# Linear attention with two MLP layers on one core: a new order of the opening and of the first block, k scaled by GpSimd, three gate buffers

## The chip, the core and the metric

The kernel runs on one core of a Trainium2 chip. A core has TensorE (matmuls, here PE; its weight loads are PEld), VectorE (DVE), ScalarE (ACT), GpSimd (POOL) and SyncE (SP, which here only issues DMAs). The metric is the device time of one execution in microseconds (us); smaller is better.

## The reference

Eight heads of a linear attention with a decaying state over 768 positions and four batches, then two MLPs on the 3072 tokens of 384 features, with 2048 hidden units each:

```python
for t in range(S):
    state = alpha[:, :, t, :, None] * state + np.einsum('bhd,bhe->bhde', k[:, :, t], v[:, :, t])
    y[:, :, t] = np.einsum('bhd,bhde->bhe', q[:, :, t], state)
# x = y as (tokens, heads * head_dim)
h = x @ w_in;  g = h * (1.0 / (1.0 + np.exp(-1.702 * h)));  x = g @ w_out
h = x @ w_in2; g = h - np.tanh(h);                          out = g @ w_out2
```

## The kernel before

**Attention.** It works in 24 chunks of 128 positions (4 batches of 6), g = 0 to 23. For a chunk VectorE makes two running products of alpha (`a_scan`, lines 258 and 261) and multiplies k by the one (line 265) and q by the other (line 266), in `a_scale`. TensorE makes the scores in two parts (`s_mm`, line 294, banks 5, 6, 3 and 4); ScalarE copies them out (line 306, and the turned k at line 303) and GpSimd masks them (line 308); then TensorE makes the outputs (`a_out`, lines 356 and 349) and the step of the state (`a_delta`, line 370), which VectorE adds (`a_state`). ScalarE copies the outputs (`a_evac`, line 414), DMAs take them to memory and back in the MLP's layout (`a_back`, line 429), and ScalarE and VectorE split them into a high and a low part (`x_hi`, line 436, and `x_lo`, line 440). A guard (`a_guard`, line 270) squares the running products on ScalarE. Chunks 2 and 3 of the opening go round the memory: placing matrices, copied by GpSimd out of the identity (`a_picks`, line 396), lay them by TensorE (`a_lay`, line 400).

**MLPs.** 3072 tokens are six blocks of 512 for each layer; a block is 16 steps, one for each 128 hidden units. A step is nine matmuls `gemm1` (line 453; high x high, high x low, low x high of three pieces of 128 features), an activation on ScalarE into a gate buffer (`gf`, in layer 1 line 467), its split into `ghi` (line 470) and `glo`, and, three steps later, nine matmuls `gemm2` (line 460). Steps are s = 0 to 191. In the first block the low part is made by ScalarE's negated copy (line 472) and a DMA that GpSimd issues and that adds the gate buffer to it (line 473); later VectorE makes it (line 475). Step s uses gate buffer s mod 2.

**Weights.** 64-bit weights of a step come by DMA (`given`, line 162). VectorE makes a 32-bit number of them (`w_bits`, lines 172 and 173, and `w_join`, line 185); ScalarE rounds it to the high part (`w_hi`, line 204) and VectorE subtracts for the low part (`w_lo`, line 208).

**The order.** Every engine works its instructions in the order in which the program writes them (`in_order` pins this for layer 1's first blocks). The opening computes chunks 0 to 3 and the weights of steps 0 and 1, with `idle` matmuls as fill (line 613). The first block then carries chunks 4 to 7 with it: one of three parts of a chunk (scores, scores, outputs) in each step from step 2, a weight in each step (`conv`: the low part of one weight, then the join of the next, then the bits of the one after), and the chunk's guard.

## Time and profile before

| | us |
|---|---|
| median of 3 runs | 932.02 (929.82 to 932.99) |
| the profiled execution | 934.48, its span 932.80 |
| TensorE busy | 912.6 (98%) |
| VectorE busy | 661.1 (71%) |
| ScalarE busy | 454.6 (49%) |
| GpSimd busy | 107.5 (12%) |

The profile is of one execution. Its page has busy times, the span in 40 slices of 23.3 us, and the granted clock of TensorE in tenths; beside it the trace answers with timelines (an x16 behind a row says how many instructions of one kind are merged in it; the first number is the start of the first, the second the busy time of all), waits, and a table by stretches of time. A busy TensorE is not one at its peak: matmuls are pipelined, and at half the granted clock the same matmul lasts longer.

### The profile page before, as it was taken

To read this page: it belongs to the slowest core of one execution; us is meant where nothing else is said; L and a number is where in the kernel's file an instruction comes from. 1 tells how busy PE (TensorE), PEld (TensorE's weight loads), DVE (VectorE), ACT (ScalarE), POOL (GpSimd) and SP (SyncE) were. 2 spreads that over 40 slices of the span, in tenths; PEclk is the share of its full clock that TensorE was granted. 3 is DMA by queue.
4 is the path that set the end of the run, shared out by engine and by line. 5 is a ranking of instruction groups with operands and counts; after the bars stand their busy time and mean duration, and the time that the engine had idled before them with its cause. 6 is when DMAs were issued, how large, how long until landed. Compare 5 with 4: busy or idle time off the path is not lost.

```text
span 932.8 us, 13408 instructions
## 1 busy us (share of the span) xinstructions
PE 912.6 (98%) x4949; PEld 720.5 (77%) x4949; DVE 661.1 (71%) x1114; ACT 454.6 (49%) x923; POOL 107.5 (12%) x98
## 2 busy tenths in 40 slices
PE   8899989999999999999999999999999999999996
PEld 5567768778777777787888888888888888888885
DVE  8799856747675674767499966766777777666663
ACT  5466634344343433434445645545655656545552
POOL 6023311101111111110100201002001001000000
PEclk9989989999999999999999999999999999999999
DMA  9979735433341632346344300200423410000001
GB/s 230 296 213 267 189 94 155 121 115 120 93 126 57 171 127 89 119 130 220 112 141 165 136 0 1 103 1 2 158 79 115 156 68 1 35 1 1 34 1 39
DMA packets 58763, 99.81 MB, mean 107 GB/s; under 512 B 5136, under 2 KB 36240, under 8 KB 58688
## 3 DMA queue, kind: packets, MB, share of 16 engines
q1 hardware_dynamic: 56096, 94.40, 31.6%
q0 software_dynamic: 2304, 4.20, 2.7%
q8 instruction: 41, 0.67, 0.3%
q10 hardware_dynamic: 288, 0.26, 0.1%
q14 instruction: 34, 0.28, 0.1%
HBM read 80.88 MB, written 13.76 MB: 101 GB/s over the span
## 4 chain that ended last, share of the span: by engine, by line
PE 93%; DMA 2%; DVE 2%; issue 1%; ACT 1%; POOL 0%; SPq 0%; POOLq 0%; ACTq 0%
PE bank L460 43%; PE bank L453 42%; PE bank L356 2%; PE bank L323 2%; PE bank L613 1%; PE bank L349 1%; PE bank L294 1%; DMA glo<-gt 1%; PE bank L370 1%; DMA given<-w 1%; DMA xt<-wtb 1%; DMA xlo<-xt 0%; DVE w L208 0%; SPq L419 0%; DVE xs L173 0%
## 5 line engine op out<-in xcount | busy, mean ns | idle before, releaser
L453 PE MATMUL bank<-xhi,w 128*128 128x512 f32 x1152 | 394.9, 397 | 6.1 <-ACT xhi L436 4.0
L460 PE MATMUL bank<-ghi,w 128*128 128x512 f32 x1152 | 367.4, 399 | 0.0
L453 PEld LDWEIGHTS bank<-xhi,w 128*128 128x128 f32 x1152 | 217.9, 189 | 59.4 <-ACT xhi L436 5.0
L460 PEld LDWEIGHTS bank<-ghi,w 128*128 128x128 f32 x1152 | 212.9, 188 | 53.2 <-issue 2.3
L475 DVE TENSOR_TENSOR glo<-gt,ghi 128x512 fp32r<-128x512 f32 x176 | 125.2, 711 | 149.9 <-ACT ghi L470 147.2
L453 PE MATMUL bank<-xlo,w 128*128 128x512 f32 x576 | 229.5, 398 | 0.7 <-DVE xlo L440 0.7
L460 PE MATMUL bank<-glo,w 128*128 128x512 f32 x576 | 228.0, 396 | 0.0
L470 ACT CAST ghi<-gt 128x512 fp32r<-128x512 f32 x192 | 119.1, 620 | 210.9 <-DVE gt L486 129.4
L453 PEld LDWEIGHTS bank<-xlo,w 128*128 128x128 f32 x576 | 109.1, 189 | 27.8 <-DVE xlo L440 1.3
L460 PEld LDWEIGHTS bank<-glo,w 128*128 128x128 f32 x576 | 108.2, 188 | 26.4
L467 ACT ACTIVATE gt<-bank 128x512 f32<-128x512 f32 x96 | 57.5, 599 | 122.5 <-PE bank L453 103.7
L484 DVE SCALAR_TENSOR_TENSOR arena<-arena,bank 128x512 f32<-128x512 f32 x96 | 65.7, 684 | 32.2 <-ACT arena L482 31.0
L482 ACT ACTIVATE arena<-bank 128x512 f32<-128x512 f32 x96 | 57.3, 596 | 39.3 <-PE bank L453 38.8
L486 DVE SCALAR_TENSOR_TENSOR gt<-arena 128x512 f32<-128x512 f32 x96 | 68.3, 711 | 9.8
L483 ACT ACTIVATE arena<-arena,cs 128x512 f32<-128x512 f32 x96 | 69.6, 725 | 2.9
L485 DVE SCALAR_TENSOR_TENSOR arena<-arena 128x512 f32<-128x512 f32 x96 | 67.9, 707 | 3.1
L523 POOL TENSOR_TENSOR xlo<-arena,xhi 128x512 fp32r<-128x512 f32 x18 | 28.3, 1599 | 339.3 <-ACT xhi L522 339.3
L333 DVE STREAM_TRANSPOSE cf<-arena 32x128 f32<-32x128 f32 x176 | 53.2, 302 | 2.5
L181 ACT ACTIVATE wtb<-wtb 128x768 bf16<-128x768 int16 x32 | 26.8, 837 | 43.3 <-DVE wtb L179 42.1
L440 DVE TENSOR_TENSOR xlo<-xlo,xhi 128x384 fp32r<-128x384 f32 x22 | 13.2, 601 | 38.9 <-ACT xhi L436 38.9
L265 POOL TENSOR_TENSOR arena<-arena 112x512 f32<-112x512 f32 x11 | 13.5, 1224 | 105.4 <-DVE seg L259 86.9
L333 DVE STREAM_TRANSPOSE cf<-raw 32x128 f32<-32x128 f32 x80 | 24.2, 302 | 1.1
(140 smaller groups left out, 669.6 us busy)
## 6 DMA issues: line engine op xcount, KB each, us to landing
raw<-w SPq DMA_DIRECT2D x48, 768.0 KB, 4.6
given<-w SPq DMA_DIRECT2D x16, 768.0 KB, 9.2
arena<-xq SPq DMA_DIRECT2D x32, 224.0 KB, 5.0
x1t<-xs SPq DMA_DIRECT2D x6, 768.0 KB, 6.5
arena<-x1t SPq DMA_DIRECT2D x6, 768.0 KB, 4.4
out<-xs SPq DMA_DIRECT2D x17, 256.0 KB, 2.3
xlo<-xt SPq DMA_DIRECT2D x22, 192.0 KB, 2.6
glo<-gt POOLq DMA_DIRECT2D x16, 256.0 KB, 5.9
```

The source lines that it names most:

```text
L333: V.transpose(out=d[32 * y : 32 * y + 32], in_=k[32 * x : 32 * x + 32, :, 32 * y : 32 * y + 32])
L453: P.matmul(out=h, lhsT=w[m][:, ws], rhs=x[:, k, :n], start=c == 0, stop=c == 3 * KT - 1)
L460: P.matmul(out=acc[k][:, :n], lhsT=w[m][:, ws], rhs=x[s % 3][:, :n], start=m == 0 and c == 0, stop=m == MT - 1 and c == 2)
L467: A.activation(out=gf[i][:, :n], in_=h, func=AF.Silu, scale=1.702)
L470: A.copy(ghi[s % 3][:, :n], gf[s % 2][:, :n])
L475: e.tensor_tensor(out=glo[s % 3][:, :n], in0=gf[s % 2][:, :n], in1=ghi[s % 3][:, :n].bitcast(F32), op=ALU.subtract)
L482: A.activation(out=u, in_=h, func=AF.Square, accum_out=usum[:, s - NS1 :][:, :1])
L483: A.activation(out=w, in_=u, func=AF.Square, bias=pbias)
L484: V.scalar_tensor_tensor(out=p, in0=u, scalar=P3, in1=h, op0=ALU.mult, op1=ALU.mult)
L485: V.scalar_tensor_tensor(out=p, in0=u, scalar=-PR, in1=p, op0=ALU.add, op1=ALU.mult)
L486: V.scalar_tensor_tensor(out=gf[i], in0=w, scalar=PD, in1=p, op0=ALU.add, op1=ALU.mult)
L523: G.tensor_tensor(out=xlo[i][:, k], in0=xr[:, k], in1=xhi[i][:, k].bitcast(F32), op=ALU.subtract)
```

## The change

1. **Opening.** `a_picks` is cut into three parts written at three places, and ScalarE makes half of its copies. The first fill is shorter (14 to 12 idle matmuls; then 2, 1 and 1 where 4, 3 and 5 stood). Each chunk's guard moves behind the first splits. The loads of chunks 4, 5 and 6 move behind weights: SP asks for the weights of steps 3 and 4 before chunk 4.
2. **k scaled by GpSimd.** For chunks 0 to 4 line 265 runs on GpSimd, where it was VectorE's (from chunk 8 on both multiplies already are GpSimd's).
3. **First block.** Chunk 4 is prepared in step 2 of the block and not ahead of it. A part of a chunk can stand behind a step's `gemm1` or behind its `gemm2` (`units`, with the table `slots`): the scores of chunk 4 now follow step 4's `gemm2`. A step makes high and low part of the weight of step m+2 and then bits and join of that of step m+3.
4. **Three gate buffers**: step s uses buffer s mod 3.
5. **The last copy** of VectorE goes to another tile (`xr`, where `xs` was).

```diff
-    gf = [gt[:, i * NB : (i + 1) * NB] for i in range(2)]
+    gf = [gt[:, i * NB : (i + 1) * NB] for i in range(3)]
...
-        e.tensor_tensor(out=qkk(g), in0=qkk(g), in1=dec3(g, 0)[:, :, :C], op=ALU.mult)
+        (G if g < 5 else e).tensor_tensor(out=qkk(g), in0=qkk(g), in1=dec3(g, 0)[:, :, :C], op=ALU.mult)
...
+                    if n:
+                        A.copy(o, w)
+                    else:
+                        G.tensor_copy(o, w)
...
-    a_picks()
-    for g in range(4):
+    a_picks(0)
+    for g in range(2):
         eye(g)
     for r in range(3):
         prep(0, r)
+    a_picks(1)
+    for g in range(2, 4):
+        eye(g)
...
+    a_picks(2)
+    idle(12)
...
         if g < 2:
+            if g:
+                a_back(0)
             a_evac(g, 0)
-            a_guard(g)
-            if g:
-                a_back(g - 1)
             w_given(g + 1)
-        if g == 0:
-            a_load(4)
+        if g == 2:
+            a_take(2, 0)
     a_back(1)
     w_given(3)
+    w_given(4)
+    w_bits(1, 1)
+    x_hi(0)
     w_hi(1, 0)
-    x_hi(0)
-    w_bits(1, 1)
-    w_join(1, 1)
...
     a_lay(3, bank[5])
     a_delta(3)
     idle(3)
-    x_hi(1)
-    w_hi(1, 1)
+    w_join(1, 1)
     w_lo(1, 0)
+    a_guard(0)
     x_lo(0)
-    x_lo(1)
-    w_lo(1, 1)
     x_hi(2, bank[6])
     x_lo(2, bank[6])
+    x_hi(1)
+    x_lo(1)
+    w_hi(1, 1)
     x_hi(3, bank[5])
     x_lo(3, bank[5])
+    w_lo(1, 1)
+    a_load(4)
+    w_given(5)
+    w_given(6)
     a_guard(2)
+    a_guard(1)
     a_guard(3)
     a_load(5)
...
     w_bits(1, 2)
     w_join(1, 2)
-    w_hi(1, 2)
-    w_lo(1, 2)
-    prep(4, 0)
-    prep(4, 1)
-    a_state(3)
-    prep(4, 2)
-    w_bits(1, 3)
-    cv[:] = 4, 3, 3
+    cv[:] = MT, MT, MT
...
+    slots = ((9, 10, 12), (13, 15, 16), (18, 19, 21), (22, 24, 25))
+
+    def units(m, half):
+        for q in range(4):
+            for r in range(3):
+                if slots[q][r] == 2 * m + half:
+                    attend(4 + q, r)
+                    if r == 1:
+                        prep(4 + q, 3)
+                    if r == 2:
+                        a_done(4 + q)
+                        a_state(4 + q)
...
+                if m in (8, 10, 13, 15):
+                    a_x(4 + (8, 10, 13, 15).index(m))
+                if m + 2 < MT:
+                    w_hi(1, m + 2)
+                    w_lo(1, m + 2)
+                if m + 3 < MT:
+                    w_bits(1, m + 3)
+                    w_join(1, m + 3)
+                if m == 2:
+                    prep(4, 0)
+                    prep(4, 1)
+                    a_state(3)
+                    prep(4, 2)
+                    a_load(6)
...
-    V.tensor_copy(xs[:, 2, half:n], acc[2][:, half:n])
+    V.tensor_copy(xr[:, 2, half:n], acc[2][:, half:n])
```

GpSimd in the opening, before: the placing copies (line 396), then the masks (line 308) of the four chunks, two each, then the DMAs of the first block (`glo`).

```order
L396 COPY cf_84<-cs 48x16
L396 COPY wtb<-cs 48x48
L396 COPY wtb<-cs 48x32
L396 COPY wtb<-cs 48x48
L308 ISA
L308 AFFINE_SELECT arena<-arena 128x512 x8
L473 DMA glo_93<-gt 128x512
L473 DMA glo_94<-gt 128x512
L308 AFFINE_SELECT arena<-arena 128x512
```

And now; line 265 is the scaling of k, line 403 a placing copy.

```order
L403 COPY cf_84<-cs 48x48 x2
L265 ISA
L265 TENSOR_TENSOR arena<-arena 112x512
L403 COPY cf_84<-cs 48x48
L403 COPY cf_84<-cs 48x16
L308 AFFINE_SELECT arena<-arena 128x512 x2
L403 COPY wtb<-cs 48x32
L265 TENSOR_TENSOR arena<-arena 112x512
L308 AFFINE_SELECT arena<-arena 128x512 x2
L265 TENSOR_TENSOR xs<-xs,gt 112x512
L308 AFFINE_SELECT arena<-arena 128x512 x2
L265 TENSOR_TENSOR raw<-raw 112x512
```

The four scalings now stand in GpSimd's row, each but the first directly behind the masks of the chunk before.

VectorE from the last weight of the opening on, before; `cf` and `xs` hold weights' numbers, `arena` and `seg` a chunk's running products (the scans at lines 258 and 261 read as SCALAR_TENSOR_TENSOR here).

```order
L172 TENSOR_SCALAR cf_84<-given_65 128x768
L173 SCALAR_TENSOR_TENSOR cf_84<-given_65,cf_84 128x768
L185 SCALAR_TENSOR_TENSOR cf_84<-given_65,cf_84 128x768
L208 TENSOR_TENSOR w_477<-cf_84,w_477 128x768
L257 MEMSET seg 112x4
L258 SCALAR_TENSOR_TENSOR arena<-arena,seg 112x516
L259 RECIPROCAL seg<-arena 112x4
L261 SCALAR_TENSOR_TENSOR arena<-arena,seg 112x516
L379 TENSOR_TENSOR state<-bank_112,state 112x192
L380 TENSOR_TENSOR state<-state,arena 112x192
L265 TENSOR_TENSOR arena<-arena 112x512
L266 TENSOR_TENSOR arena<-arena 112x4x128
```

And now:

```order
L208 TENSOR_TENSOR w_443<-cf_83,w_443 128x768
L172 TENSOR_SCALAR cf_84<-given_65 128x768
L173 SCALAR_TENSOR_TENSOR cf_84<-given_65,cf_84 128x768
L185 SCALAR_TENSOR_TENSOR cf_84<-given_65,cf_84 128x768
L208 TENSOR_TENSOR w_474<-cf_84,w_474 128x768
L172 TENSOR_SCALAR xs<-given_66 128x768
L173 SCALAR_TENSOR_TENSOR xs<-given_66,xs 128x768
L185 SCALAR_TENSOR_TENSOR xs<-given_66,xs 128x768
L208 TENSOR_TENSOR w_494<-xs,w_494 128x768
L172 TENSOR_SCALAR xs<-given_67 128x768
L173 SCALAR_TENSOR_TENSOR xs<-given_67,xs 128x768
L185 SCALAR_TENSOR_TENSOR xs<-given_67,xs 128x768
```

Chunk 4's preparation (lines 257 to 266) is gone from here, three weights later; a weight's bits, join and low part (lines 172, 173, 185 and 208) now follow each other, and the low part of weight 1 has come in from ahead of the activations.

SP's DMAs from chunk 0's outputs on, before: `xt<-` takes a chunk's outputs to memory, `xlo<-xt` brings them back, `given` are weights, `arena<-xq` and `arena<-xv` the loads of a chunk.

```order
L419 DMA xt<-arena 48x2x128 x4
L162 DMA given_64<-w 128x1536
L251 DMA arena<-xq 112x516
L251 DMA arena<-xq 112x512
L251 DMA arena<-xq 112x4x128
L251 DMA arena<-xv 128x384
L419 DMA xt<-wtb 48x2x128 x4
L429 DMA xlo_87<-xt 128x3x128
L162 DMA given_65<-w 128x1536
L429 DMA xlo_87<-xt 128x3x128
```

And now:

```order
L426 DMA xt<-arena 48x2x128 x4
L162 DMA given_64<-w 128x1536
L436 DMA xlo_87<-xt 128x3x128
L426 DMA xt<-wtb 48x2x128 x4
L162 DMA given_65<-w 128x1536
L436 DMA xlo_87<-xt 128x3x128
L162 DMA given_66<-w 128x1536
L162 DMA given_67<-w 128x1536
L251 DMA arena<-xq 112x516
```

The loads of chunk 4 have moved from ahead of chunk 1's outputs to behind the weights of steps 3 and 4.

## Rows read from the trace of the kernel before

**Rows 1.** The page, part 2: busy tenths and granted clock in 40 equal slices.

```profile
PE   8899989999999999999999999999999999999996
...
PEclk9989989999999999999999999999999999999999
```

**Rows 2.** The table by stretches: us from:to, length, busy of each engine, clock.

```profile
36.03:96.95 60.92, 56.21 (x336) 42.43 (x337) 55.84 (x77) 35.68 (x80) 13.90 (x16) 0.92 0.90 259
120.85:124.47 3.62, 0.01 (x2) 0.00 (x1) 0.02 (x1) 1.05 (x3) 0.00 (x0) 0.77 0.93 273
124.47:130.27 5.80, 5.80 (x25) 4.15 (x25) 4.44 (x12) 1.59 (x3) 2.04 (x2) 0.55 0.25 45
```

**Rows 3.** The waits of TensorE: who waited for whom, total us, times, longest.

```profile
PE bank L453 <- ACT xhi L436: 4.0, 2, 3.6
```

**Rows 4.** Chain of waits (start, us, what) and ScalarE's timeline, end of block one.

```profile
115.07 8.26 DMA glo<-gt
...
123.42 0.60 ACT L467 ACTIVATE gt<-bank 128x512 f32<-128x512 f32 x1 [5.75 <-DMA glo<-gt]
```

**Rows 5.** Timeline of the opening: start, us, engine, line, instruction, [idle before <-releaser].

```profile
5.97 1.23 DVE L261 TENSOR_TENSOR_SCAN arena<-arena,seg 112x516 f32<-112x516 f32 x1
...
7.12 0.67 DVE L265 TENSOR_TENSOR arena<-arena 112x512 f32<-112x512 f32 x1
...
8.49 1.47 PE L294 MATMUL bank<-arena 48*128 48x176 f32 x16 [0.31 <-issue]
...
9.36 1.25 ACT L306 COPY arena<-bank 128x256 f32<-128x256 f32 x4 [1.81 <-PE bank L294]
...
13.05 1.47 PE L294 MATMUL bank<-arena 48*128 48x176 f32 x16
...
17.23 1.46 PE L294 MATMUL bank<-xs 48*128 48x176 f32 x16 [0.37 <-ACT arena L414]
...
19.93 1.73 POOL L308 TENSOR_SCALAR_AFFINE_SELECT arena<-arena 128x512 f32<-128x512 f32 x2 [2.31 <-ACT arena L306]
...
22.30 1.47 PE L294 MATMUL bank<-raw 48*128 48x176 f32 x16 [0.76 <-ACT wtb L414]
...
25.14 1.27 POOL L308 TENSOR_SCALAR_AFFINE_SELECT arena<-arena 128x512 f32<-128x512 f32 x2 [3.47 <-ACT arena L306]
...
26.99 1.08 PE L356 MATMUL bank<-arena,raw 128*48 128x128 f32 x16
...
31.19 1.60 PE L400 MATMUL bank<-wtb,cf 112*128 112x128 f32 x12 [0.55 <-ACT wtb L409]
...
34.92 0.50 PE L453 MATMUL bank<-xhi,w 128*128 128x512 f32 x1 [0.43 <-ACT xhi L436]
...
36.09 0.50 PE L453 MATMUL bank<-xlo,w 128*128 128x512 f32 x1 [0.67 <-DVE xlo L440]
```

**Rows 6.** Timeline at the end of block one: GpSimd's multiplies and VectorE beside them.

```profile
108.49 1.51 POOL L265 TENSOR_TENSOR arena<-arena 112x512 f32<-112x512 f32 x1
108.62 3.35 DVE L208 TENSOR_TENSOR w<-xs,w 128x768 fp32r<-128x768 f32 x1
...
129.02 1.18 POOL L265 TENSOR_TENSOR raw<-raw 112x512 f32<-112x512 f32 x1 [2.41 <-DVE raw L258]
```

**Rows 7.** Timeline inside block one, then VectorE's group of low parts by form.

```profile
38.52 0.83 ACT L204 CAST w<-cf 128x768 fp32r<-128x768 f32 x1 [1.55 <-DVE cf L185]
...
45.02 1.54 PE L294 MATMUL bank<-arena 48*128 48x176 f32 x8 [2.63 <-DVE arena L266]
...
96.26 0.69 DVE L266 TENSOR_TENSOR arena<-arena 112x512 f32<-112x512 f32 x1
...
97.78 0.87 PE L294 MATMUL bank<-arena 48*128 48x176 f32 x8
...
L208 DVE TENSOR_TENSOR w<-cf,w 128x768 fp32r<-128x768 f32 x10 | 9.5, 949 | 2.8 <-ACT w L204 2.8
```

**Rows 8.** Timeline of the last copies and their DMA.

```profile
925.92 0.42 DVE L813 COPY xs<-bank 128x256 f32<-128x256 f32 x1 [1.81 <-ACT xs L812]
```

More of the change, by code (lines that the diff above doesn't have):

```diff
@@ L385, in linear_attention_mlps, with a_picks @@
     picks = [(k, b, a) for k in range(KT) for a in range(2) for b in range(2) if (k, a) not in ((0, 1), (2, 0))]
-    def a_picks():
-        for n in (cf[2][:DP], wtb[:DP, NP * C :]):
-            G.memset(n, 0.0)
+    def a_picks(part):
+        if not part:
+            for n in (cf[2][:DP], wtb[:DP, NP * C :]):
+                G.memset(n, 0.0)
         for i, (k, b, a) in enumerate(picks):
             for n in range(2):
+                if i // 3 != part:
+                    continue
                 at = D * (2 * n + b + 4 * a) - C * k
@@ L463, in linear_attention_mlps, with gb @@
     HB = [bank[3], bank[4]]
+    turn = [3]
+    def gb(s):
+        return gf[s % turn[0]]
     def sig_1(s, h, n):
-        i = s % 2
-        A.activation(out=gf[i][:, :n], in_=h, func=AF.Silu, scale=1.702)
+        A.activation(out=gb(s)[:, :n], in_=h, func=AF.Silu, scale=1.702)
     def g_split(s, n, e):
-        A.copy(ghi[s % 3][:, :n], gf[s % 2][:, :n])
+        A.copy(ghi[s % 3][:, :n], gb(s)[:, :n])
         if e is G:
-            A.activation(out=glo[s % 3][:, :n], in_=gf[s % 2][:, :n], func=AF.Copy, scale=-1.0)
-            G.dma_start(out=glo[s % 3][:, :n].bitcast(F32), in_=gf[s % 2][:, :n], accum_op=ALU.add)
+            A.activation(out=glo[s % 3][:, :n], in_=gb(s)[:, :n], func=AF.Copy, scale=-1.0)
+            G.dma_start(out=glo[s % 3][:, :n].bitcast(F32), in_=gb(s)[:, :n], accum_op=ALU.add)
             return
-        e.tensor_tensor(out=glo[s % 3][:, :n], in0=gf[s % 2][:, :n], in1=ghi[s % 3][:, :n].bitcast(F32),
+        e.tensor_tensor(out=glo[s % 3][:, :n], in0=gb(s)[:, :n], in1=ghi[s % 3][:, :n].bitcast(F32),
                         op=ALU.subtract)
@@ L485, in tanh_near @@
         V.scalar_tensor_tensor(out=p, in0=u, scalar=-PR, in1=p, op0=ALU.add, op1=ALU.mult)
-        V.scalar_tensor_tensor(out=gf[i], in0=w, scalar=PD, in1=p, op0=ALU.add, op1=ALU.mult)
+        V.scalar_tensor_tensor(out=gb(s), in0=w, scalar=PD, in1=p, op0=ALU.add, op1=ALU.mult)
     def tanh_1(s, h, n):
         i = 0
-        hs, u, w, p, d, mk, g = f_hs[i], f_u[i], f_w[i], f_p[i], f_d[i], f_m[i], gf[s % 2]
+        hs, u, w, p, d, mk, g = f_hs[i], f_u[i], f_w[i], f_p[i], f_d[i], f_m[i], gb(s)
         A.activation(out=u, in_=h, func=AF.Square)
@@ L501, in tanh_2 @@
     def tanh_2(s):
-        V.copy_predicated(gf[s % 2], f_m[0], f_d[0])
+        V.copy_predicated(gb(s), f_m[0], f_d[0])
     def evac(l, t0, n, acc, ks=range(KT)):
@@ L640, in linear_attention_mlps @@
         s_copy(0, x % 2, (5, 3)[x % 2], x > 1)
-    idle(14)
+    a_picks(2)
+    idle(12)
     for g in range(4):
@@ L654, in linear_attention_mlps @@
         if g < 3:
-            idle((4, 3, 5)[g])
-            for x in range(2):
-                s_copy(g + 1, x, (5, 3)[x], False)
-            if g == 2:
-                a_take(g, 0)
-            for x in range(2):
-                s_copy(g + 1, x, (5, 3)[x], True)
+            idle((2, 1, 1)[g])
+            for x in range(4):
+                s_copy(g + 1, x % 2, (5, 3)[x % 2], x > 1)
         if g < 2:
+            if g:
+                a_back(0)
             a_evac(g, 0)
-            a_guard(g)
-            if g:
-                a_back(g - 1)
             w_given(g + 1)
-        if g == 0:
-            a_load(4)
+        if g == 2:
+            a_take(2, 0)
     a_back(1)
     w_given(3)
+    w_given(4)
+    w_bits(1, 1)
+    x_hi(0)
     w_hi(1, 0)
-    x_hi(0)
-    w_bits(1, 1)
-    w_join(1, 1)
     a_lay(2, bank[6])
@@ L796, in linear_attention_mlps @@
                 evac(l, t0, n, acc)
+            if s < MT:
+                units(s, 1)
         if s == (len(L1) - 1) * MT - 1:
@@ L812, in linear_attention_mlps @@
     A.copy(xs[:, 2, :half], acc[2][:, :half])
-    V.tensor_copy(xs[:, 2, half:n], acc[2][:, half:n])
+    V.tensor_copy(xr[:, 2, half:n], acc[2][:, half:n])
     A.dma_start(out=out[2, :, t0 : t0 + half], in_=xs[:, 2, :half])
-    SP.dma_start(out=out[2, :, t0 + half : t0 + n], in_=xs[:, 2, half:n])
+    SP.dma_start(out=out[2, :, t0 + half : t0 + n], in_=xr[:, 2, half:n])
     in_order(since)
+    turn[0] = 2
     bad = nc.values_load(flag, min_val=0, max_val=1)
```

22 lines of the change are left out of this document (5 added, 17 removed).

## The prediction

> **What bounds the kernel now.** I read the page first, TensorE's busy share and granted clock by slices [rows 1]. From the seventh slice (140 us) to the last but one both stand at 9, the highest digit, so what VectorE, ScalarE or a DMA does later can hardly move the end. The change can be worth something only before 140 us, and a little behind the last matmul. The busy share is at 8 in slices 1, 2 and 6, the clock in 3 and 6. There I read the table by stretches, TensorE's waits, and then the timeline of one engine at a time.
>
> Three losses show. (a) At the end of the first block TensorE stands still from 120.85 to 124.47, 3.62 us, and then works 5.80 us at a granted clock of 0.55 [rows 2]; that clock costs 5.80 x 0.45 = 2.6 us more. TensorE's longest wait is for ScalarE's split of x [rows 3], but ScalarE itself was held 5.75 us in front of it, in the activation that writes a gate buffer, by a GpSimd-queued DMA that still read the buffer: issued at 115.07, 8.26 us until it was done [rows 4]. (b) The opening: the first chunks go through VectorE, GpSimd, TensorE and ScalarE in turn; the first matmul that uses the last low part of the activations starts at 36.09 [rows 5]. (c) Early in the block TensorE waits 2.63 us for chunk 4's scaled q and restarts at half rate [rows 7].
>
> **The change part by part.** I follow the path in four pieces and compare each piece's length.
>
> *Three gate buffers.* The activation of step s now needs the DMA of step s-3 done, not s-2. In the rows the late DMA was issued at 115.07; with a third buffer the activation of step 15 asks for the one before it, issued a step earlier, and the late one has until the activation of step 16, nine matmuls later at least. From 115.07 to 120.85 are 5.8 us, and the next product and chunk 8's scores lie behind that, so the 8.26 us that it took fit. The split of chunk 7 then runs at once behind the activation, about 1 us of ScalarE and 0.6 us of VectorE, under the nine matmuls of the next-to-last product. I take away the 3.62 us and the 2.6 us of low clock that follow a stop: **-6.2**. What is late next is the low half of the same step, which the DMA brings; TensorE asks for it a step later. In the other blocks TensorE does not wait, so the third buffer is worth nothing there. The later halves of the change in this block (chunk parts between the products of a step) move matmuls but add none: from the first score matmul of chunk 7, at 97.78 [rows 7], to the stop at 120.85 [rows 2] lie 23.07 us of back-to-back matmuls, and the same matmuls stand there after the change. I keep 23.07.
>
> *The opening, with k scaled by GpSimd.* VectorE loses one multiply of 0.67 us for each of the first four chunks [rows 5]; GpSimd gets it. On GpSimd the same multiply (rows of later chunks) takes 1.18 us alone and 1.51 us beside VectorE [rows 6]. More important is its place: GpSimd works in order, and the scaling of chunk g+1 now stands behind the two masks of chunk g, which wait for ScalarE's copies of scores of chunk g. So the score matmuls of g+1 can't start before them. The masks of a chunk are done 4.43 us (17.23 to 19.93 + 1.73) or 4.11 us (22.30 to 25.14 + 1.27) after its score matmuls start [rows 5]. A cycle is so 4.1 to 4.4 plus 1.18 to 1.51, that is 5.3 to 5.9 us. Before, the three starts were 4.18 and 5.07 us apart (13.05, 17.23, 22.30).
> The first cycle: chunk 0's second scan ends at 7.20, GpSimd's scaling in the way of VectorE's multiply of q gives 7.20 + 1.18 + 0.67 = 9.05 for the first score matmul (8.49 before). Copies start 0.87 us after it and take 1.25 us, the last mask 0.86, the scaling 1.18: chunk 1 starts at 13.2. The placing copies, of which ScalarE now does half, don't hold GpSimd any more. But GpSimd and VectorE get in each other's way; if a scan of 1.23 us comes between twice, it is 15.7. Chunk 3 starts two cycles on, between 13.2 + 10.6 = 23.8 and 15.7 + 11.8 = 27.5. From there: 4.1 us to its masks, then the path from 26.99 to 36.09 without its waits. That is 9.1 us less 0.55, 0.43 and 0.94 (34.92 to 36.09 but for one matmul of 0.23), 7.2 us [rows 5]. The loads of chunk 4 no longer stand ahead of the DMAs that take chunk 1 out and back, which is why I take these waits away. So 36.09 becomes 35.1 to 38.8. I take the middle, 37.0: neither end is a row, since no row has the scaling at this place. **+0.9** (-1.0 to +2.7).
> The guards (four activations on ScalarE) move behind; they now lie under the first products, where ScalarE waits anyway. The idle matmuls that go were fill for waits; they cost nothing and save nothing.
>
> *From the first product to chunk 7's scores.* Before, 36.03 to 97.78. The stretch ends with VectorE: it finishes chunk 7's q at 96.95, and the score matmul starts 0.8 us behind, when its product is through [rows 7]. VectorE was busy 55.84 of these 60.92 us [rows 2]. After the change it does more before that point: one weight's low part comes after the activations, not before, and one weight's low part and one combining step more stand ahead of chunk 7's q, 3 x 0.95 = 2.85 us (the row of the low part; the other has a like size); the multiply that GpSimd took saves 0.69 but GpSimd holds VectorE for it, 1.18 to 1.51. And each of weights 2, 3, 4 and 6 is now worked on in one go: bits, combine, ScalarE's cast, low part, with nothing of VectorE's in between, so that VectorE stands through the cast, 0.83 us plus hand-over [rows 7], 4 x 0.87 = 3.5. Sum 55.84 + 2.85 - 0.69 + 1.3 + 3.5 = 62.8. Of the 5.08 us that VectorE waited before, most were behind ScalarE held by the gate buffers or behind a weight's DMA; I keep 0 to 3.4 of them, so 62.8 to 66.2, and take 64.3. Chunk 7's scores now start right at that end: 64.3 against 61.75. **+2.5** (+1.0 to +4.4). So the loss (c) goes only in name: TensorE's early wait for chunk 4 becomes smaller waits for weights, and VectorE is the bound of the block. Chunk 4's scaling also stands ahead of the DMA of step 2's low half in GpSimd's row and waits for VectorE's scan; that DMA goes out late, but TensorE asks for it only behind chunk 4's scores, which wait for the same scan. Chunk 4's later place costs no more than this, because the wait of the scores of chunk 5 takes it in.
>
> *The tail.* VectorE's last copy waited until 925.92 for ScalarE's copy into the same tile; it takes 0.42 us itself [rows 8], and ScalarE's has the other half of the tile to copy. In another tile it need not wait, and the last DMA can be issued a copy earlier: **-0.4** (0 to -0.4).
>
> **Sum.** -6.2 + 0.9 + 2.5 - 0.4 = -3.2 us. The profiled execution took 934.48 us (span 932.80), so it would be 931.3; the median of the runs is 932.02, 2.46 below the profiled one, which gives 928.8. The sum of the good ends is -6.2 - 1.0 + 1.0 - 0.4 = -6.6 (925.4), that of the bad ends -6.2 + 2.7 + 4.4 - 0.4 = +0.5 (932.5).
>
> **The rivals.** *GpSimd and VectorE shut each other out in full.* For it: one subtraction of VectorE that takes 0.95 us took 3.35 us while GpSimd did its two multiplies [rows 6]. Against it: a pair of masks took 1.73 us in the thick of VectorE's scans, 1.27 us at a quieter time [rows 5], so a mask loses only some tenths. If all of it is added up, both bad ends hold: 932.5, no change.
> The Trainium skill has this as a rule in "SBUF — State Buffer", in the part on the shared port pair: GpSimd and a VectorE instruction with two SBUF inputs take one port pair by an exclusive lock, and the other "fully blocks". By that rule the bad ends hold and 932.5 would come out; the trace agrees with it in the 3.35 us, less in the masks.
>
> *The clock falls in the opening: slower.* Between the filler behind chunk 0's scores and chunk 1's there are now 12 matmuls of 0.23 us. They end at 9.05 + 1.47 + 2.8 = 13.3, and chunk 1 may start at 15.7, 2.4 us later. After a stop of 2.63 us the clock was at half (eight score matmuls 1.54 us at 45.02, 0.87 at 97.78) [rows 7]; the 0.76 us and shorter stops of the opening did nothing. At half rate each chunk's scores cost 2 x 0.67 = 1.3 us more and the half of its outputs that the copies wait for about 0.5, so 1.8 us in each of three cycles, 5.5 us, and two chunks' placing matmuls and outputs 2 us more: 928.8 + 7.5 = 936.3. It decides as soon as the stops in the opening come to what preceded the low clock at 45.02. Against it: VectorE, freed of 0.67 us for each chunk, may be out of GpSimd's way by then.
>
> *The stop at the end stays.* If the DMA queue is still behind when step 15 wants its buffer, or the DMA that brings chunk 7 back is late, half of (a) comes back: 928.8 + 3.1 = 931.9.
>
> *The change does more than I say*: GpSimd and VectorE don't meet, and ScalarE never lags: 925.4.
>
> **How the numbers follow.** Two executions of this kernel differ by up to 0.3%, 2.8 us, so below 929.2 is faster and above 934.8 is slower. Forecast: 0.48, its own range 926.5 to 931.5, two thirds of it below 929.2 (0.32 faster, 0.16 same). Better than forecast, 925.4: 0.12. Shut out in full, 932.5: 0.17. Stop stays, 931.9: 0.07. Clock falls, 936.3: 0.16. Faster 0.44, same 0.40, slower 0.16. The range goes from the sum of the good ends to near the slow rival, 925.4 to 935.0; what is left out is most of the slow rival and a little below.
>
> **What would show it.** Right: no TensorE wait near the end of the first block and a full clock across it; the first product some 1 us later than now; GpSimd's scaling followed at once by score matmuls; VectorE busy to over 90% from the first product to chunk 7's q, with four casts waited for. Wrong: score matmuls of chunk 3 at 22 us or earlier (GpSimd is not the bound of the opening), TensorE waiting for weights less than 2 us in the block (VectorE is not), or a granted clock near 0.5 between 13 and 37 us (the slow rival).

## The result and the profile after

The changed kernel is slower: 936.21 us (median of 22 runs, 932.89 to 939.24) against 931.56 us (22 runs, 927.36 to 934.50). The ratio is 1.0054, with a 95% interval of 1.0041 to 1.0067, so +5.0 us. The forecast was 928.8 us with a range up to 935.0; the time came out above the range, in the place of the slow rival (936.3). The profiled execution after took 937.82 us (span 936.0), the one before 934.48 (span 932.8).

The page of the changed kernel, part 2 (busy tenths and granted clock in 40 slices), beside [rows 1]:

```profile
PE   6979999999999999999999999999999999999997
...
PEclk8889999999999999999999999999999999999999
```

The sixth slice, the end of the first block, is now full; the loss sits in the first three slices. The table by stretches (us from:to, length, then busy time of TensorE, its weight loads, VectorE, ScalarE and GpSimd, granted clock, DMA share, GB/s) shows both; its last two lines are the stretch in which TensorE stood still before [rows 2], and the one in which the changed kernel comes to the same place of its work, ahead of chunk 8 and into it:

```profile
15.00:20.00 5.00, 4.54 (x36) 4.10 (x38) 2.19 (x2) 1.01 (x3) 0.60 (x2) 0.54 0.75 230
20.00:25.00 5.00, 3.21 (x30) 2.22 (x28) 4.09 (x6) 1.65 (x8) 3.18 (x3) 0.50 0.32 66
25.00:30.00 5.00, 4.90 (x57) 3.43 (x55) 0.55 (x2) 2.01 (x8) 1.99 (x3) 0.59 0.48 170
120.85:124.47 3.62, 3.62 (x17) 2.96 (x16) 2.05 (x4) 2.36 (x5) 0.78 (x1) 1.00 1.07 217
128.00:134.00 6.00, 6.00 (x38) 4.70 (x37) 4.07 (x11) 2.75 (x5) 1.58 (x2) 1.00 0.78 185
```

So the third gate buffer did what it was taken for: TensorE is busy in the whole of both stretches, at full clock. In the opening, 15 us ran near a clock of 0.5, where the kernel before had 1.00 throughout. TensorE's waits (who waited for whom, total us, times, longest) have new names against [rows 3]:

```profile
PE bank L467 <- DMA glo<-gt: 3.5, 1, 3.5
PE bank L294 <- POOL arena L265: 2.1, 1, 2.1
PE bank L294 <- DVE seg L257: 1.8, 1, 1.8
PE bank L294 <- POOL xs L265: 1.8, 1, 1.8
...
PE bank L294 <- issue: 1.4, 1, 1.4
PE bank L460 <- ACT w L204: 1.4, 1, 1.4
```

The timeline of the opening, with the same columns as [rows 5] (line 265 scales k, 308 masks, 294 is a score matmul, 403 a placing copy that stayed on GpSimd):

```profile
5.97 1.17 POOL L265 TENSOR_TENSOR arena<-arena 112x512 f32<-112x512 f32 x1
5.99 2.23 DVE L261 TENSOR_TENSOR_SCAN arena<-arena,seg 112x516 f32<-112x516 f32 x1
...
9.21 1.47 PE L294 MATMUL bank<-arena 48*128 48x176 f32 x16 [1.82 <-DVE seg L257]
...
10.81 2.38 POOL L308 TENSOR_SCALAR_AFFINE_SELECT arena<-arena 128x512 f32<-128x512 f32 x2 [2.44 <-ACT arena L306]
...
13.14 1.13 POOL L403 COPY wtb<-cs 48x32 f32<-48x32 f32 x1
...
14.24 1.17 POOL L265 TENSOR_TENSOR arena<-arena 112x512 f32<-112x512 f32 x1
...
15.46 2.72 PE L294 MATMUL bank<-arena 48*128 48x176 f32 x16 [2.06 <-POOL arena L265]
...
23.45 2.72 PE L294 MATMUL bank<-xs 48*128 48x176 f32 x16 [1.78 <-POOL xs L265]
...
30.48 1.47 PE L294 MATMUL bank<-raw 48*128 48x176 f32 x16 [0.57 <-POOL raw L265]
```

Here is the loss. Chunk 3's scores start at 30.48 instead of 22.30. Between chunk 0's and chunk 1's scores GpSimd does two masks, a placing copy and the scaling in a row; the 12 filler matmuls end 2.06 us before that row does, and from there the score matmuls take 2.72 instead of 1.47 us. The first matmul on a last low part starts at 41.75 (36.09 before).

Inside the first block, three lines answer to [rows 7] and [rows 4]: VectorE's last scaling of chunk 7 and the score matmuls that follow it, and (from the chain of waits, start, us, what) the DMA that TensorE waited 3.5 us for:

```profile
47.09 9.83 DMA glo<-gt
...
105.37 0.69 DVE L266 TENSOR_TENSOR arena<-arena 112x512 f32<-112x512 f32 x1
...
106.16 0.87 PE L294 MATMUL bank<-arena 48*128 48x176 f32 x8 [1.44 <-issue]
```

And the tail, for [rows 8]: VectorE's last copy has another tile, and waits as before.

```profile
929.54 0.42 DVE L838 COPY arena<-bank 128x256 f32<-128x256 f32 x1 [1.87 <-ACT xs L837]
```

Four marks carry the comparison of all kernels below: the start of chunk 3's scores, of the first matmul on a low part, of chunk 7's scores, and of chunk 8's first whole-chunk matmuls (line 323 in every kernel) at the end of the first block. From the last mark to the end of the span lie 803.2 us in the changed kernel and 804.0 before: all of the difference arises ahead of it. "old" and "new" stand for the kernel before and the changed one; ratios are to the kernel before in the same session, where its median was between 929.6 and 931.6 us. A difference in us beside a ratio is the ratio less 1, times 931.6; the difference of the plain medians can be about a microsecond off it.

| kernel | ratio (95%) | median us | chunk 3 | low part | chunk 7 | chunk 8 |
|---|---|---|---|---|---|---|
| before | 1 | 931.56 | 22.30 | 36.09 | 97.78 | 128.77 |
| changed | 1.0054 (1.0041 to 1.0067) | 936.21 | 30.48 | 41.75 | 106.16 | 132.77 |
| third gate buffer alone | 0.9969 (0.9952 to 0.9985) | 927.94 | 22.56 | 37.49 | 98.59 | 123.70 |
| changed, k on VectorE | 0.9978 (0.9962 to 0.9994) | 929.29 | 22.62 | 33.88 | 98.35 | 124.98 |
| the same, second session | 0.9983 (0.9968 to 0.9999) | 929.83 | 22.79 | 34.07 | 98.53 | 125.13 |
| changed, old opening | 1.0003 (0.9985 to 1.0020) | 930.90 | 22.49 | 35.69 | 100.03 | 125.10 |
| changed, more filler | 1.0046 (1.0028 to 1.0064) | 935.11 | 27.71 | 40.25 | 104.65 | 129.71 |
| changed, scaling ahead of masks | 1.0014 (0.9998 to 1.0031) | 931.45 | 23.62 | 34.90 | 99.37 | 124.43 |
| the same, second session | 0.9998 (0.9982 to 1.0015) | 931.15 | 24.32 | 35.67 | 100.43 | 127.04 |
| old order, third buffer, k on GpSimd | 1.0042 (1.0022 to 1.0062) | 934.95 | 34.50 | 46.01 | 107.75 | 132.85 |
| changed, old block | 1.0012 (0.9995 to 1.0030) | 931.84 | 28.00 | 39.27 | 101.36 | 126.47 |
| changed, old block, k on VectorE | 0.9958 (0.9938 to 0.9978) | 926.31 | 22.67 | 33.94 | 95.95 | 121.06 |
| the same, second session | 0.9956 (0.9941 to 0.9972) | 926.11 | 22.93 | 34.21 | 95.53 | 120.64 |
| changed, k on VectorE, early load | 0.9997 (0.9978 to 1.0016) | 930.11 | 23.01 | 36.12 | 101.58 | 126.64 |

### The profile page after: what moved, and what is told of

It is laid out like the page before. It is cut to its first block, busy times and chain, and to the rows that moved or that the text cites. A ratio compares the mean times of both kernels' runs of the same rounds, so it can differ in the third digit from the quotient of the medians.

```text
span 936.0 us, 13423 instructions
## 1 busy us (share of the span) xinstructions
PE 913.7 (98%) x4939; PEld 723.1 (77%) x4939; DVE 658.4 (70%) x1109; ACT 457.0 (49%) x928; POOL 109.0 (12%) x98
## 4 chain that ended last, share of the span: by engine, by line
PE 95%; DMA 1%; POOL 1%; DVE 1%; ACT 1%; issue 1%; ACTq 0%; POOLq 0%; DVEq 0%
PE bank L467 44%; PE bank L460 42%; PE bank L356 2%; PE bank L323 2%; PE bank L294 2%; PE bank L349 1%; DMA glo<-gt 1%; PE bank L370 1%; ACT arena L306 0%; POOL arena L308 0%; PE bank L407 0%; DMA arena<-xq 0%; DVE arena L261 0%; POOL xs L265 0%; DVE arena L258 0%
## 5 line engine op out<-in xcount | busy, mean ns | idle before, releaser
L265 POOL TENSOR_TENSOR arena<-arena 112x512 f32<-112x512 f32 x14 | 16.6, 1188 | 112.3 <-DVE seg L259 68.9
```

## The experiments

The theory after the result: the third buffer's gain is real, and k on GpSimd takes more than it back in the opening. The rivals: the fewer filler matmuls (the clock) do it, or the new order of the first block.

**The third gate buffer alone.**

```diff
-    gf = [gt[:, i * NB : (i + 1) * NB] for i in range(2)]
+    gf = [gt[:, i * NB : (i + 1) * NB] for i in range(3)]
...
-        A.activation(out=gf[i][:, :n], in_=h, func=AF.Silu, scale=1.702)
+        A.activation(out=gb(s)[:, :n], in_=h, func=AF.Silu, scale=1.702)
```

> The kernel before with the third gate buffer alone; nothing else of the change. Theory (the buffer's gain was real and is hidden by losses elsewhere): the stop of 3.62 us at 120.85 and the 2.6 us of low clock behind it go, ratio about 0.9935, some 925.5 against 931.6. Rival (the wait only changes its name, because chunk 7 or the DMA of the low half is late anyway): ratio 0.998 to 1.001, and another wait of 2 us or more stands between 115 and 128.

Measured 0.9969, -2.9 us (-4.5 to -1.4): between the two. ScalarE's activation in the profile no longer waits for a DMA but, briefly, for the product before it, and TensorE is busy throughout:

```profile
119.60 0.60 ACT L471 ACTIVATE gt<-bank 128x512 f32<-128x512 f32 x1 [1.12 <-PE bank L453]
...
120.00:125.00 5.00, 5.00 (x34) 3.87 (x33) 4.16 (x11) 2.35 (x5) 0.85 (x1) 1.00 1.08 284
```

So the wait didn't change its name; the rival falls as a mechanism. From chunk 7's scores to chunk 8 the profile shows 25.11 us instead of 30.99, 5.9 us less, which is the size forecast. Yet the ratio gives half of it (the plain medians of that session, 931.62 and 927.94, lie 3.7 us apart).

**The kernel before, two more profiles.** Nothing is edited.

> The kernel before, unchanged, profiled once more. Question: is the stop at the end of its first block (3.62 us in the profile that the prediction rests on, an execution 2.9 us above the median) there in every execution? Theory: no; where the execution is near or under the median of 931.6 the stop is under 1.5 us or absent and chunk 8's first whole-chunk matmuls stand near 125, not 128.77. Rival: the stop is always 3 us or more, and the third buffer alone gains less than the stop for another reason.

> The kernel before, unchanged, profiled a third time, with the same question and the same numbers: a stop under 1.5 us where the execution is near or under the median (theory), 3 us or more whatever the time (rival).

They took 931.70 and 933.27 us; the other runs of the kernel before in that session have a median of 929.62. The chain of waits and TensorE's timeline at the stop, then the table over the 5.80 us behind it, of the first:

```profile
114.46 7.07 DMA glo<-gt
...
122.65 0.50 PE L453 MATMUL bank<-xhi,w 128*128 128x512 f32 x1 [2.32 <-ACT xhi L436]
...
122.65:128.45 5.80, 5.70 (x27) 4.22 (x28) 4.85 (x13) 1.60 (x3) 2.05 (x2) 0.71 0.41 77
```

and of the second:

```profile
114.14 8.16 DMA glo<-gt
...
123.43 0.79 PE L453 MATMUL bank<-xhi,w 128*128 128x512 f32 x1 [3.42 <-ACT xhi L436]
...
123.43:129.23 5.80, 5.79 (x25) 4.21 (x25) 4.45 (x12) 1.60 (x3) 2.03 (x2) 0.54 0.26 47
```

With [rows 2] and [rows 4] there are three executions of one program: DMA 8.26, 8.16 and 7.07 us; stop 3.6, 3.4 and 2.3; clock in the 5.80 us behind it 0.55, 0.54 and 0.71; chunk 8 at 128.77, 127.74 and 126.06; and 934.48, 933.27 and 931.70 us in all. The size of the stop varies with one DMA, and the execution's time goes with it: the last two of these move together within 0.2 us. From chunk 7's scores to chunk 8 these executions took 30.99, 30.80 and 28.79 us; without what lies above the 25.11 us of the third buffer they would have taken 928.6, 927.6 and 928.0 us, about the median with it, 927.94. The theory's number (under 1.5 us near the median) was not met, since 2.3 us were left at 931.70, and so was not the rival's. Which stop the median execution has no profile shows: all three lie above the medians of the runs beside them, by 2.9, 3.7 and 2.1 us. But 29 of the 32 runs of the kernel before in the session of the third buffer lie above all 12 runs with it (925.8 to 930.0 us, against 926.3 to 934.5).

**k back on VectorE.**

```diff
-        (G if g < 5 else e).tensor_tensor(out=qkk(g), in0=qkk(g), in1=dec3(g, 0)[:, :, :C], op=ALU.mult)
+        e.tensor_tensor(out=qkk(g), in0=qkk(g), in1=dec3(g, 0)[:, :, :C], op=ALU.mult)
```

> The changed kernel with one line undone: k of the first five chunks is scaled by VectorE again. Theory (the scaling on GpSimd, in a row behind the masks, makes the chunk cycle of the opening long and lets the clock fall): chunk 3's scores start near 23 instead of 30.48, the granted clock from 15 to 30 is 1.00, the first low-part matmul near 36.5 instead of 41.75, and the ratio to the kernel before comes down from 1.0054 by some 5.2 of 931.6, to 0.999 or 1.000. Rival (the fewer filler matmuls and the other order of the opening do it without GpSimd): low clock between 15 and 30 stays, chunk 3 at 28 or later, ratio 1.004 or more.

> The changed kernel with k on VectorE once more, beside the next two on one chip. Theory: ratio 0.996 to 0.999, as in its first run (0.9978).

Measured 0.9978 and 0.9983. This one line costs 0.0074, about 6.9 us, in the changed kernel, and without it the change would have been a small gain. TensorE's timeline and clock:

```profile
17.55 1.46 PE L294 MATMUL bank<-xs 48*128 48x176 f32 x16 [1.01 <-ACT arena L421]
...
22.62 1.47 PE L294 MATMUL bank<-raw 48*128 48x176 f32 x16 [1.19 <-ACT wtb L421]
...
15.00:20.00 5.00, 3.99 (x66) 3.08 (x64) 4.89 (x8) 2.83 (x13) 2.08 (x2) 1.00 1.03 289
```

The filler is the changed kernel's, 12, 2, 1 and 1, and the clock stays at 1.00: stops of 1.2 us and less did nothing to it. The filler alone is not the cause.

**The old opening in the changed kernel** (its order, its filler, k of chunks 0 to 3 on VectorE, that of chunk 4 still on GpSimd, with the loads and weights handed over where the new block expects them).

> The changed kernel with the opening of the kernel before (its order, its filler, k of chunks 0 to 3 on VectorE, all picks by GpSimd); the first block's new order, three gate buffers and the tail stay. Theory (the whole loss is made in the opening, 5.7 us, and the block loses 2.7 and wins 4.4 in itself): first low-part matmul near 36, ratio near 0.9995. Rival (the block's new order is what costs, so that a sooner opening only waits longer for weights and chunk 4): first low-part matmul near 36, but chunk 7's scores still at 104 or later and ratio 1.003 or more.

Measured 1.0003, as the theory said, and the rival's mark fails too, with chunk 7 at 100.03. But the old opening is 2.3 thousandths behind the new one with k on VectorE (0.9980, mean of two): the first low part at 35.69 against 33.88. So the rest of the new order of the opening looks like a gain of some 2 us, about the scatter of such a difference.

**More filler.**

```diff
-    idle(12)
+    idle(20)
...
-            idle((2, 1, 1)[g])
+            idle((12, 11, 10)[g])
```

> The changed kernel with more filler matmuls in the opening only: 20 instead of 12 behind chunk 0's scores, and 12, 11 and 10 instead of 2, 1 and 1 behind the outputs of chunks 0 to 2; k stays on GpSimd. Theory A (the clock is what the longer chain costs): granted clock 1.00 from 10 to 35, score matmuls 1.47 us, cycles of 5.5 to 6.2 instead of 7.99 and 7.03, chunk 3's scores at 26.5 to 28 instead of 30.48, ratio 1.0015 to 1.003. Theory B (the chain GpSimd, TensorE, ScalarE alone costs it, the clock is only seen beside it): clock 1.00, yet chunk 3 at 29.5 or later and ratio 1.0045 or more.

Measured 1.0046, -0.8 thousandths against the change, within its scatter: theory B by the time, theory A by the marks. In the profile the clock is full and the cycles are 6.26, 6.05 and 5.98 us:

```profile
15.00:20.00 5.00, 4.67 (x58) 3.22 (x57) 3.77 (x5) 2.31 (x10) 2.23 (x4) 1.00 0.90 251
...
21.73 1.46 PE L294 MATMUL bank<-xs 48*128 48x176 f32 x16 [0.49 <-POOL xs L265]
...
27.71 1.47 PE L294 MATMUL bank<-raw 48*128 48x176 f32 x16
...
33.49 1.08 PE L356 MATMUL bank<-arena,raw 128*48 128x128 f32 x16
...
25.62 1.18 POOL L265 TENSOR_TENSOR raw<-raw 112x512 f32<-112x512 f32 x1
```

Chunk 3 at 27.71 lies between k on VectorE (22.62) and the change (30.48): 5.1 us with the clock kept up, 2.8 the low clock on top. But the filler itself holds TensorE: chunk 3's scaling is done at 26.80, 0.9 us before the filler is, and the matmuls at 33.49 start 5.78 us behind chunk 3's scores instead of 4.50 in the change, 1.3 us later. So by this profile the chain through GpSimd makes some 4.2 us at chunk 3 and the low clock 3.7, and 2.2 us of filler lie in the time of this run and hide most of what the clock gave back (the first low part is at 40.25, the change's at 41.75). A filler that ends with the wait was not tried.

**The scaling ahead of the masks.** In GpSimd's row the scaling of chunk g+1 goes before the masks of chunk g:

```diff
+    for r in range(3):
+        prep(1, r)
     for x in range(4):
         s_copy(0, x % 2, (5, 3)[x % 2], x > 1)
...
-            for r in range(3):
-                prep(g + 1, r)
...
             idle((2, 1, 1)[g])
+            for r in range(3):
+                if g < 2:
+                    prep(g + 2, r)
```

> The changed kernel with one move: in GpSimd's row the scaling of k of chunk g+1 stands ahead of the masks of chunk g, not behind them; VectorE's row is the same, k stays on GpSimd. Theory A (it is the place in GpSimd's row that makes the opening long): cycles back to 4.2 to 5.1 us, chunk 3's scores at 23 to 25, granted clock full, ratio 0.998 to 1.000. Theory B (GpSimd is a slow place for this multiply, and it stretches VectorE's scans): chunk 3 at 27 or later, ratio 1.003 or more.

> The changed kernel with GpSimd's scaling ahead of the masks once more, beside k on VectorE on the same chip. Theory A (the place in GpSimd's row is nearly all of the cost; the traces have the first product of the first block at 34.48 against 33.46): 1 us above k on VectorE or level with it. Theory B (GpSimd and VectorE in each other's way are a cost of their own, as the first runs, 1.0014 and 0.9978, say): 2.5 us or more above it.

Measured 1.0014, then 0.9998 beside 0.9983 for k on VectorE on the same chip, medians 1.3 us apart; the first pair, 1.0014 and 0.9978, is 3.4 us apart and above theory A's range. That is theory A by the marks and by the second pair, but for a remainder of a microsecond or more. GpSimd's timeline and chunk 3's scores:

```profile
10.30 1.18 POOL L265 TENSOR_TENSOR arena<-arena 112x512 f32<-112x512 f32 x1 [1.96 <-DVE arena L258]
11.44 2.60 POOL L308 TENSOR_SCALAR_AFFINE_SELECT arena<-arena 128x512 f32<-128x512 f32 x2
13.99 1.13 POOL L403 COPY wtb<-cs 48x32 f32<-48x32 f32 x1
15.21 1.19 POOL L265 TENSOR_TENSOR xs<-xs,gt 112x512 f32<-112x512 f32 x1
...
23.62 1.47 PE L294 MATMUL bank<-raw 48*128 48x176 f32 x16 [1.03 <-ACT wtb L421]
```

The same instructions on the same engine, and chunk 3 comes 6.9 us sooner (23.62 against 30.48; 24.32 in the second session): the place in the row was the cost, not the engine. What is left, 1.0 us against k on VectorE, is where GpSimd and VectorE meet; the pair of masks takes 2.60 us here and 1.27 at a quiet time [rows 5].

**k on GpSimd in the old order**, with the third buffer, one line as above but for chunks 0 to 3 only.

> The kernel before with the third gate buffer, and k of chunks 0 to 3 scaled by GpSimd, behind the masks as in the change; the opening keeps its old order and its old filler (14, then 4, 3 and 5 matmuls), the block its old order. Theory (the scaling on GpSimd is what costs, whatever the order around it): 5 to 7 us above the third buffer alone, ratio 1.002 to 1.005, cycles of 6 us and more in the opening. Rival (it costs only together with the change's own order and its 12, 2, 1 and 1 fillers): ratio under 1.000.

Measured 1.0042, 7.0 us above the third buffer alone: the theory. The old filler didn't save it:

```profile
13.68 2.72 PE L294 MATMUL bank<-arena 48*128 48x176 f32 x16 [5.66 <-POOL arena L265]
...
21.31 1.47 PE L294 MATMUL bank<-arena 48*128 48x176 f32 x16
...
27.36 2.72 PE L294 MATMUL bank<-xs 48*128 48x176 f32 x16 [2.24 <-POOL xs L265]
...
34.50 1.47 PE L294 MATMUL bank<-raw 48*128 48x176 f32 x16
```

Here chunk 0's scaling also stands behind all ten placing copies, which GpSimd has done by 11.44, hence 13.68. The change had given half of these copies to ScalarE and spread the rest, which is why its own first chunk lost only 0.7 us. So the 7 us here and those of the change are not made up alike: chunk 0 has 4.9 of them already (13.68 against 8.76).

**The old block in the changed kernel**, once with k on GpSimd and once on VectorE (weights in the old order, chunk parts in whole steps, chunk 4 prepared in the opening). In a first form the load of chunk 6 stood ahead of chunk 3's guard, which then squared chunk 6's values in their shared place and held ScalarE until the load was there; these times (1.0077 and 1.0009) are of another computation and decide nothing.

> The changed kernel with the first block of the kernel before (weights in the old order, chunk parts in whole steps, chunk 4 prepared in the opening, its k on VectorE); new opening with k of chunks 0 to 3 on GpSimd and three gate buffers stay. Theory (parts add up: the new block costs 0.0034, from the old opening with the new block, 1.0003, less the third buffer alone, 0.9969): ratio about 1.0020, first score matmuls of chunk 3 still near 30. Rival (parts don't add up, the late opening is half hidden by something in one of the blocks): ratio under 1.000 or over 1.004.

> As the kernel with the old block, and k of all chunks on VectorE again: new opening without GpSimd, old block, three gate buffers. Theory (parts add up: k on VectorE in the changed kernel gave 0.9978, the new block costs 0.0034): ratio about 0.9944, better than the third buffer alone (0.9969). Rival (the rest of the new opening is worth nothing; what k on VectorE won over the old opening was scatter): 0.9965 to 0.998.

In the second form the load stands behind the guard.

> The changed kernel with the first block of the kernel before, the load of chunk 6 now behind chunk 3's guard; new opening with k of chunks 0 to 3 on GpSimd and three gate buffers stay. Theory (parts add up: the new block costs 0.0034): ratio about 1.0020, chunk 3's scores near 30. Rival (they don't): under 1.000 or over 1.004.

> The same with k of all chunks on VectorE: new opening without GpSimd, old block, three gate buffers. Theory (parts add up): ratio about 0.9944, better than the third buffer alone (0.9969). Rival (the rest of the new opening is worth nothing): 0.9965 to 0.998.

> New opening with k on VectorE, old block, three gate buffers, once more, on the same chip as k on VectorE with the new block. Theory: ratio 0.994 to 0.997 and 2 to 3.5 us under k on VectorE with the new block, which is then the price of the new block. Rival (the new block costs nothing of itself): within 1 us of it.

Measured 1.0012 with k on GpSimd (theory 1.0020; chunk 3 at 28.00, in a profile in which the clock fell less), and 0.9958 and 0.9956 with k on VectorE (theory 0.9944, its rival 0.9965 to 0.998: between them, and the intervals take in both; the second session's own theory, 0.994 to 0.997, holds). On one chip the new block is 3.7 us behind the old one, 929.83 against 926.11 (2 to 3.5 expected). This is also the fastest version found, about 4.0 us under the kernel before (the third buffer alone, 0.9969, is not clearly apart from it): three gate buffers, the new order of the opening, k on VectorE, the old block. Chunk 8's whole-chunk matmuls start at 121.06, about when TensorE came to its stop before [rows 2].

**Chunk 4's load early again.** With k on VectorE TensorE still waits 3.18 us in the new block for the DMA of a low half (3.5 us in the change). The load of chunk 4 and chunk 0's guard, on which it waits, go back behind chunk 0's outputs.

```diff
+            if not g:
+                a_guard(0)
             w_given(g + 1)
+            if not g:
+                a_load(4)
...
-    a_guard(0)
...
-    a_load(4)
```

> k on VectorE as in the run with 0.9978, and chunk 0's guard and the load of chunk 4 back at their old place behind chunk 0's outputs, the other guards stay late. Theory (the wait of 3.18 us for the DMA of the low half in the first block comes from loads that were held until the late guard and then run together with it): DMA share from 20 to 35 up from 0.72 and 0.83 to about 1, that wait under 1.5 us, ratio 0.995 to 0.9965. Rival (the wait comes from the weights that are now fetched a step sooner): wait 2.5 us or more, ratio 0.997 to 0.999.

Measured 0.9997: no gain, rather a loss of 1.7 thousandths. The wait did shrink as the theory said, and the activations came later instead; TensorE's timeline has both:

```profile
35.53 0.49 PE L460 MATMUL bank<-xhi,w 128*128 128x512 f32 x1 [1.31 <-ACT xhi L443]
...
51.17 0.50 PE L467 MATMUL bank<-glo,w 128*128 128x512 f32 x1 [0.81 <-DMA glo<-gt]
```

The DMA engines look like the shared resource (share 1.09 instead of 0.83 from 25 to 30 us, and over 1 from 35 to 60 in both): what the late load gave to the first product, some 2 us, it took from the DMA of the low half, and the other way round. This is read from the rows and was not tried apart.

## Why the prediction was wrong

With the third buffer, three switches were turned separately: order of the opening, engine of k, order of the block. In thousandths of the time, by the ratios, the third buffer is -3.1; k on GpSimd +7.3 (old opening, old block), +5.5 (new, old) and +7.4 (new, new); the new block +3.4, +2.3 and +4.2; the new order of the opening without GpSimd -1.2 and -2.3, with it -3.0. Each difference carries about 2 of scatter. Along one path: -3.1 - 1.2 + 2.3 + 7.4 = +5.4, the change.

*Three gate buffers, -6.2: mechanism right, size wrong.* The stop and the low clock went, and profile against profile of the buffer alone the block's end is 5.9 us shorter. By the ratio it is -2.9 (-4.5 to -1.4). The step that failed is the passage from the profiled execution to the median: the stop was measured in an execution 2.9 us slower than the median, and -2.46 were then taken off the sum once more for that same slowness. By the further profiles the stop is what makes such an execution slow, so these microseconds were counted twice.

*The opening, +0.9 (-1.0 to +2.7): wrong, the main miss.* Its order without GpSimd gained 1.2 to 2.3 thousandths, 1 to 2 us; k on GpSimd cost 5 to 7 us. In the marks of the profile the first low part is 5.66 us late. Two steps failed.

The first is the sentence that the placing copies don't hold GpSimd any more: one of 1.13 us stands between the masks and the scaling of chunk 1, and the masks took 2.38 us where one of 0.86 was counted behind the copies. (That each scaling but the first stands directly behind the masks, as the section on the change has it, does not hold for chunk 1; the list above that sentence shows the copy between.) The first cycle became 6.25 us, at the upper end of what was allowed for (chunk 1 at 15.46, bounds 13.2 to 15.7), and behind this stop the clock fell.

The second is that the forecast priced the two later cycles at full clock, 5.3 to 5.9 us each, and left the low clock to a rival of chance 0.16. They took 7.99 and 7.03 us. With the clock kept up they took 6.05 and 5.98, the last with 0.9 us of filler in it, so without the clock they were about as priced. Chunk 3 came 4.8 us behind the middle of the forecast (25.65); 2.8 to 3.7 of these are the low clock, the rest mostly the first cycle. The middle of a range was taken whose lower end needed GpSimd and VectorE to stay out of each other's way; the masks beside scans (1.73 against 1.27 us for a pair [rows 5]) spoke for the upper one.

*The slow rival.* It named the place, the mechanism and nearly the stop (2.4 us forecast, 2.06 measured); its condition, a stop like the 2.63 us before 45.02, was not reached, and the clock fell all the same. The total of 936.3 fits by chance: the low clock was priced at 7.5 us and is worth 2.8 to 3.7 at chunk 3, and some 3 us in time, an estimate from the 1.1 us between the medians of the change and of more filler and the 2.2 us that the filler held. "Against it: VectorE may be out of GpSimd's way" did not hold: VectorE waits for outputs of TensorE itself, with 2.2, 4.1 and 0.6 us of work in the three slow stretches of 5 us.

*The shut-out.* A scan that starts with GpSimd's scaling takes 2.23 instead of 1.23 us, a lengthening of about the multiply beside it (1.17). So the trace agrees, for these rows, with the rule of the Trainium skill, "SBUF — State Buffer", in the part on the shared port pair, that the other one "fully blocks". The reverse shows too, in the timeline of the changed kernel, where the scan starts first and the multiply takes 2.13 us:

```profile
21.18 1.23 DVE L258 TENSOR_TENSOR_SCAN raw<-raw,seg 112x516 f32<-112x516 f32 x1
21.26 2.13 POOL L265 TENSOR_TENSOR xs<-xs,gt 112x512 f32<-112x512 f32 x1
```

The run with the scaling ahead of the masks puts what this does at 1 to 1.6 us (first low part against k on VectorE, 34.90 to 33.88 and 35.67 to 34.07), and at 1.3 and 3.4 us by the times. The expensive thing was not the shared pair but the place in an in-order row.

*From the first product to chunk 7's scores, +2.5: right in size, by errors that cancel.* From first low part to chunk 7 lie 64.41 us after and 64.47 with k on VectorE (forecast 64.3, before 61.7), and the scores follow VectorE's scaling by 0.1 us, so VectorE is the bound there. But the terms are not those of the sum. VectorE is busy 57.9 of the 63.4 us before its last scalings (91%), 2.1 us more than before where 2.85 - 0.69 + 1.3 = 3.5 were counted; and it stands 4.1 us behind casts where it stood 3.4 before, so the 3.5 us put down for four casts were for the most part there already. TensorE's largest wait, 3.5 us, had no term: it is for the low half of step 0, whose DMA was issued at 47.09 and took 9.83 us. Before, chunk 4's scores stood ahead of the product that uses it and covered it; now they stand behind that product. The prediction spoke of step 2's low half alone.

From chunk 7's scores on the prediction kept 23.07 us to the place of the stop; to chunk 8 that makes 30.99 - 6.2 = 24.8 us. It took 25.1 in most kernels with a third buffer, and 26.6 in the change, with k on VectorE twice, and with the scaling ahead of the masks the second time. The 1.5 us are the clock. In front of chunk 7 TensorE stands 1.44 or 1.45 us in all eight profiles with the new block; behind it the clock fell to 0.66 to 0.73 over 5 us in these four, and stayed at 1.00 in the four others (old opening, more filler, the scaling ahead of the masks the first time, early load). With k on VectorE, then in the old opening:

```profile
98.35 0.87 PE L294 MATMUL bank<-arena 48*128 48x176 f32 x8 [1.44 <-issue]
...
98.00:103.00 5.00, 4.65 (x19) 3.63 (x20) 3.46 (x8) 2.73 (x8) 0.63 (x1) 0.69 0.81 225
...
100.03 0.87 PE L294 MATMUL bank<-arena 48*128 48x176 f32 x8 [1.45 <-issue]
...
100.00:105.00 5.00, 4.97 (x26) 3.94 (x26) 3.46 (x7) 3.25 (x8) 1.13 (x2) 1.00 0.62 152
```

With k on VectorE the new block is behind the old one by 2.4 us at chunk 7 (98.35 to 95.95), the +2.5 of the forecast, and by 3.9 at chunk 8 (124.98 to 121.06); in the second session by 3.0 and 4.5. The last 1.5 had no term, and as the four other profiles show, the new block does not bring it every time.

*The tail, -0.4: not there.* The copy waits 1.87 us for ScalarE's as it did (1.81), in another tile. The two copies read the same bank; whether that is what joins them was not tried.

Of the 8.2 us between -3.2 and +5.0, the third buffer makes 3.3 and the opening 4.9 (-1.2 and +7.4 thousandths are 5.8 us, less the 0.9 forecast); block and tail cancel. Of what the prediction named as signs of its being wrong, two came. One was a granted clock near 0.5 between 13 and 37 us. The other was that TensorE's waits for weights stayed under 2 us, which should have spoken against VectorE as the bound and did not: the low half took their place.

## What to carry to other kernels

Work that is moved to an engine with free time stands in that engine's row: ask what it stands behind, and what that waits for, before asking how fast the engine is. Look whether the profiled execution is a slow one, and whether the stall to be removed is what makes it slow; then its removal is worth less in the median than in the profile. When three things are changed in one order, run each alone: here one line took back more than the other parts gained.

## What the runs showed of the hardware

A DMA of 256 KB, `glo<-gt`, took from 7.07 to 9.83 us in the places shown. In three executions of one program the same one took 7.07, 8.16 and 8.26 us, the stop behind it 2.3, 3.4 and 3.6 us, and the clock in the 5.80 us behind the stop was 0.71, 0.54 and 0.55; the executions took 931.70, 933.27 and 934.48 us.

TensorE's granted clock fell to half behind a stop of 2.06 us in the opening (2.72 instead of 1.47 us for the score matmuls) and recovered only from 30 us on, with further stops between. The same stop of 2.06 us stands in the changed kernel with the old block; there the score matmuls behind it still took 1.47 us, and the clock was 0.68 from 15 to 20 us. Behind 1.44 or 1.45 us in front of chunk 7 it fell in four profiles and stayed at 1.00 in four. Behind 1.53 us in the opening, with the scaling ahead of the masks, it stayed at 1.00 in one session and was 0.66 from 20 to 25 us in the other. Stops of 1.19 us and less in the opening with k on VectorE left it at 1.00. So in these runs the length of a stop alone did not settle whether the clock fell, or when.
